# The last inverse pair of the first batch through DRAM instead of a direct table, four early units of the second batch, and low weight words on ScalarE

## The chip, the cores and the metric

The kernel runs on one core of one Trainium2 chip. The metric is the device time of one execution in microseconds (us), from three runs of the kernel before; the median is given. Profiled executions come with a trace of every instruction on TensorE (PE; its weight loads are PEld), VectorE (DVE), ScalarE (ACT), GpSimd (POOL) and SyncE (SP, which only issues DMAs).

## What is computed

```python
X = np.fft.rfft(x, axis=1)                  # x: 8 batches x 3008 rows x 256, float32
Y = X * (filt_r + 1j * filt_i)[None, :, :]
y = np.fft.irfft(Y, n=3008, axis=1).astype(np.float32)
t = y.reshape(8 * 3008, 256)                # 24064 tokens
h = t @ w_in                                # 256 -> 2048
g = h * np.clip(h + 3.0, 0.0, 6.0) / 6.0    # hard-swish
out = g @ w_out                             # 2048 -> 256
```

`w_in` and `w_out` come as float64 words; everything is computed in float32, so the kernel has to convert two 4 MB weights by itself, from pairs of 32-bit words.

## The kernel before

**Mixing.** The transform over 3008 = 47 x 64 rows is split into matrix products with small tables. For each batch after the first, `a_unit` (L433) makes the 47-point sums of four columns from `xs`, which `x_load` (L375) fetches with four SP DMAs; ScalarE copies one or both of its two PSUM banks to SBUF, `a_sums` (L447) does the rest on VectorE (for batch 1 one copy each for the last two units), and `z_store` (L456) writes the result to DRAM. `t2_load` fetches it transposed, `b_unit` (L479) makes the 64-point sums of two frequencies, `f_unit` (L499) multiplies by the filter on VectorE (three products of 128 x 512), `y_unit` (L513) adds the products, and `bi_unit` (L524) makes the inverse 64-point sums of a pair of units, which ScalarE copies out (L534) and `g_store` (L544, POOL's DMA queue) writes to DRAM (`g_tmp`). The inverse 47-point step reads it from there into `t4` and leaves tokens in the ring `xn`, of which the FFN takes blocks of 512. Batch 0 skips the first trip through DRAM: `a0_unit` (L403) and `turn` (L412, transposes on TensorE) do its first half. It also lets `bi_unit` take the filter's products directly, without `y_unit`, for all pairs but the last.

**The first block of tokens.** The first block needs only six groups of rows of batch 0. `first_load` (L575) fetches those six from `g_tmp` into `t4`, four SP DMAs at a time, for a stretch of frequencies. Frequencies 0 to 19 come this way, from the pairs that begin with units 0 to 8; for pair 8 `g0_first` (L537) writes just the six groups by four DMAs of 24 KB, two on ScalarE's queue and two on SP's. The last four frequencies (units 10 and 11) do not go through DRAM: `y_unit` adds their products on VectorE, and `direct` (L639) multiplies them by a table `direct_t` (128 x 4 x 564 float32, 1128 KB, loaded in the prologue) right into the PSUM tiles `psn`. `n_first` (L651) then adds the rest from `t4`, and ScalarE copies the result into `xn` (L658 to L662). Pair 10's inverse, wanted by later blocks only, runs between `direct` and `n_first` in the PSUM tiles `al` and `be`; pairs 8 and 10 are stored whole, on POOL's queue, after `n_first`.

**The FFN.** 47 blocks of 512 tokens, each of eight steps (256 hidden columns a step). Block 0 is multiplied plainly: `plain_up` (L784: L789, four matmuls for each half of a step), a relu on ScalarE (L726) and a product on VectorE (L731), then `plain_down` (L793: L800). Later blocks use a Strassen-Winograd form with fewer products (L681, L757), which needs sums of weights (`w_sums`, L356, 64 additions on POOL, and `w_scale`) and of tokens (`t_sums`, L671, POOL).

**Weights.** They come in 16 parts of 128 x 512 words in pairs (512 KB): `load_bits` fetches into whichever buffer is free, `w_abs` (L318) lets ScalarE take the magnitude of the high word (L321), and VectorE puts the float together (`w_conv`: L330, L332, L334 and, for the low word, L336; `w_conv_2`: L348, L350, L353). Low words are taken as a fraction between 1 and 2 by shift and mask, and L348 subtracts the 1 and multiplies. Part 0 is converted early, parts 1 to 3 between the first transform and block 0 (`w_abs` of 1 and 2 ahead of `direct`, of 3 after `n_first`), the rest in halves in steps 0 to 7 of block 0 (3, 3, 3, 4, 4, 3, 2, 2 halves). The tile of the magnitude has two buffers.

**What sets the order.** All of it is written out by hand: the whole runs under `tc.manual_schedule()`, each engine works its instructions off in the order in which the program issues them, and waits are put in for data and buffers. The prologue (L892 to L997) is straight code. From block 0 on a list `plan` holds what is done in each step; `at(step, fn, ...)` adds to it. `places(n)` (L1051) gives the steps for batch n's units; for batch 1: `a_unit` in steps 2 to 9, `b_unit` from step 12, `y_unit` from step 14. Steps 0 to 7 are block 0, 8 to 15 block 1.

Of the kernel before, what the change touches and what calls it, by code (L numbers as in the profile page):

```python
# [26 lines left out]
N = 3008  # L27
# [11 lines left out]
XC = 4  # L39
# [16 lines left out]
ATOM = 2 * KH  # L56
FIRST = tuple(range(NJ + 1, 0, -1))
# [19 lines left out]
def _make_tables():  # L77
# [76 lines left out]
    direct = np.zeros((P, TC, ND))  # L154
    for k in range(KH):
# [13 lines left out]
        if k >= KH - TC:  # L169
            for q in range(64):  # L170
                fr = k + NA * q if q < 32 else NA * (q - 31) - k
                for n, j in enumerate(FIRST):
                    th = [2 * np.pi * ((fr * rows(j, h, a)) % N) / N for h in range(2)]
                    direct[q, k - KH + TC, n * TOK:(n + 1) * TOK] = 2 / N * first_of(np.cos(th), n)
                    direct[HALF + q, k - KH + TC, n * TOK:(n + 1) * TOK] = -2 / N * first_of(np.sin(th), n)
    wai = np.concatenate([t.reshape(P, -1) for t in (groups, ones, first, last)], axis=1)
    f = np.float32
    return wa.astype(f), wai.astype(f), wb.astype(f), wi.astype(f), wf.astype(f), start.astype(f), direct.astype(f)
# [3 lines left out]
def kernel(  # L182
# [11 lines left out]
    wa_np, wai_np, wb_np, wi_np, wf_np, start_np, direct_np = _make_tables()  # L194
# [6 lines left out]
    direct_d = nc.inline_tensor(direct_np, name="direct_t").ap()  # L201
# [104 lines left out]
    def w_load(i, q):  # L306
        if W_AT[i] == "g":
            t = gp.tile([P, 7, 256], FP32, name="g")
            st["rest"] = t[:, 4:7, :].rearrange("p a n -> p (a n)")
            t = t.bitcast(I32)[:, 0:4, :].rearrange("p a n -> p (a n)")  # L310
        elif W_AT[i] == "x":
            t = xtp.tile([P, 5, PAIRS], FP32, name="xt").bitcast(I32)[:, 0:4, :].rearrange("p a n -> p (a n)")
        else:
            t = op.tile([P, 1024], I32, name="bits", tag="o")
# [3 lines left out]
    def w_abs(i):  # L318
        words = st["bits", i].rearrange("p (n two) -> p n two", two=2)
        st["high", i] = sp.tile([P, 512], FP32, name="s1")  # L320
        nc.scalar.activation(out=st["high", i], in_=words[:, :, 1].bitcast(FP32), func=AXT.Abs)  # L321


    def w_conv(i):
# [11 lines left out]
        v.tensor_scalar(out=lo, in0=lo, scalar1=9, scalar2=0x3F800000,  # L336
                        op0=ALU.logical_shift_right, op1=ALU.bitwise_or)

    def w_conv_2(i):
        big, rest, lo, hi = st.pop(("conv", i))  # L340
        v = nc.vector
        high = st.pop(("high", i), None)
        if high is None:
# [4 lines left out]
        v.scalar_tensor_tensor(out=rest, in0=lo.bitcast(FP32), scalar=1.0, in1=rest,  # L348
                               op0=ALU.subtract, op1=ALU.mult)
# [83 lines left out]
    def a_unit(b, c):  # L433
        xc = xs[:, (b * NB + c) % 3, :, :]
        t = t1p.tile([P, XC // 2, 2, D], FP32, name="t1")
        ps = [bank(b).rearrange("p (j d) -> p j d", d=D) for h in range(2)]
# [76 lines left out]
    def y_unit(b, i):  # L513
        s1, s2 = st["y", b, i]
        if b == 0 and i % 2 == 0:
            st["y0"] = t1p.tile([P, 2, 2, D], FP32, name="t1")
        y = yp.tile([P, 2, D], FP32, name="y") if b else st["y0"][:, i % 2, :, :]
# [6 lines left out]
    def bi_unit(b, i, ps=None):  # L524
        ys = [st.pop(("y", b, i + v)) for v in range(2)]
        ps = ps or [psF.tile([P, 2, D], FP32, name="psf", tag="f") for ri in range(2)]
        for v, ri in ((0, 0), (1, 0), (0, 1), (1, 1)):

            products = isinstance(ys[v], tuple)
            w, y = (wi[:, 1 + ri, :], ys[v][ri]) if products else (wi[ts(ri, 64), 0 if b else 3, :], ys[v][ts(ri, 64)])  # L530
# [6 lines left out]
    def g0_first(i):  # L537
        t = st["t3", 0, i]
        for v in range(2):
            for h in range(2):  # L540
                (nc.scalar, nc.sync)[v].dma_start(g_d[0, ds(h * HC + 1, NJ + 1), :, ds(2 * (i + v), 2), :].rearrange("c ri u d -> c ri (u d)"),
                                    t[ds(v * 64 + h * HC + 1, NJ + 1)].rearrange("p ri u d -> p ri (u d)"))

    def g_store(b, i):  # L544
        t = st.pop(("t3", b, i))
        for v in range(2):
            nc.gpsimd.dma_start(g_d[b, :, :, ds(2 * (i + v), 2), :].rearrange("c ri u d -> c ri (u d)"),  # L547
# [91 lines left out]
    def direct(i):  # L639
        if "psn" not in st:  # L640
# [547 lines left out]
```

## Time and profile before

| | us |
|---|---|
| median of 3 runs | 2660.89 (2660.49 to 2661.43) |
| the profiled execution | 2661.05 |
| its span in the trace | 2659.2 |
| TensorE busy | 2642.1 (99%) |
| VectorE busy | 2058.6 (77%) |
| ScalarE busy | 1306.3 (49%) |
| POOL busy | 495.1 (19%) |
| first matmul of block 0 (L789) | starts at 65.27 |
| first matmul of block 1 (L681) | starts at 129.30 |

The granted clock of TensorE is 1.0 over the span. A line of the page or of a group names the source line, the engine, the operation, the tile written and the tiles read; an arrow in square brackets says for how long the engine had been idle and what ended it. The chain of waits is followed back from the last instruction: each step is what released the one after it. A buffer may carry the name of an earlier tile in its place: `x0` and the direct table lie in the space of `w_all`, and so show up under that name.

### The profile page before, as it was taken

To read this page: it belongs to the slowest core of one execution; us is meant where nothing else is said; L and a number is where in the kernel's file an instruction comes from. 1 tells how busy PE (TensorE), PEld (TensorE's weight loads), DVE (VectorE), ACT (ScalarE), POOL (GpSimd) and SP (SyncE) were. 2 spreads that over 40 slices of the span, in tenths; PEclk is the share of its full clock that TensorE was granted. 3 is DMA by queue.
4 is the path that set the end of the run, shared out by engine and by line. 5 is a ranking of instruction groups with operands and counts; after the bars stand their busy time and mean duration, and the time that the engine had idled before them with its cause. 6 is when DMAs were issued, how large, how long until landed. Compare 5 with 4: busy or idle time off the path is not lost.

```text
span 2659.2 us, 54237 instructions
## 1 busy us (share of the span) xinstructions
PE 2642.1 (99%) x21584; PEld 2317.6 (87%) x21584; DVE 2058.6 (77%) x3503; ACT 1306.3 (49%) x2672; POOL 495.1 (19%) x731
## 2 busy tenths in 40 slices
PE   8999999999999999999999999999999999999999
PEld 6588888888888888888888888888888888899998
DVE  7978867877688876888768887688877878767666
ACT  3454444445545545455444545445455454454554
POOL 2252122111221112211031110311113120111110
PEclk9999999999999999999999999999999999999999
DMA  9732233212331123411223113231122421110000
GB/s 244 215 99 70 63 103 98 64 36 72 87 109 56 36 77 82 109 56 36 84 76 109 56 38 85 72 109 56 45 78 72 109 59 47 45 43 21 21 20 24
DMA packets 134818, 198.24 MB, mean 75 GB/s; under 512 B 23146, under 2 KB 99016, under 8 KB 134374
## 3 DMA queue, kind: packets, MB, share of 16 engines
q1 hardware_dynamic: 117037, 150.12, 19.8%
q0 software_dynamic: 16960, 44.16, 6.3%
q8 instruction: 170, 2.79, 0.4%
q14 instruction: 82, 0.67, 0.1%
q10 hardware_dynamic: 569, 0.50, 0.1%
HBM read 122.43 MB, written 83.98 MB: 78 GB/s over the span
## 4 chain that ended last, share of the span: by engine, by line
PE 95%; DVE 3%; DMA 1%; issue 0%; ACT 0%; SPq 0%; POOL 0%; POOLq 0%; DVEq 0%; ACTq 0%
PE po L757 43%; PE al L681 24%; PE be L681 18%; PE psn L621 2%; PE psf L531 2%; PE psf L440 2%; PE psf L487 1%; DVE g L731 1%; DMA w_all<-in_x_dram 0%; PE po L496 0%; PE po L800 0%; PE psn L632 0%; PE psf L496 0%; PE po L407 0%; DVE y L332 0%
## 5 line engine op out<-in xcount | busy, mean ns | idle before, releaser
L757 PEld LDWEIGHTS po<-w_all,g 128*128 128x128 f32 x10276 | 1362.3, 191 | 153.1 <-issue 44.1
L757 PE MATMUL po<-w_all,g 128*128 128x128 f32 x10276 | 1402.2, 276 | 0.2
L726 ACT ACTIVATE r<-h,half_c 128x512 f32<-128x512 f32 x736 | 531.0, 721 | 355.5 <-DVE h L707 343.5
L731 DVE SCALAR_TENSOR_TENSOR g<-r,h 128x512 f32<-128x512 f32 x736 | 531.3, 722 | 212.6 <-ACT r L726 200.3
L681 PE MATMUL al<-xt,w_all 128*128 128x256 f32 x2208 | 659.7, 381 | 0.1
L681 PE MATMUL be<-xt,w_all 128*128 128x256 f32 x1472 | 437.8, 379 | 0.0
L707 DVE TENSOR_TENSOR h<-be,s 128x512 f32<-128x512 f32 x368 | 253.9, 690 | 158.5 <-PE be L681 151.2
L681 PEld LDWEIGHTS al<-xt,w_all 128*128 128x128 f32 x2208 | 335.4, 192 | 1.0 <-POOL w_all L361 0.5
L681 PEld LDWEIGHTS be<-xt,w_all 128*128 128x128 f32 x1472 | 279.7, 190 | 37.9
L721 ACT ACTIVATE h<-al 128x256 f32<-128x256 f32 x368 | 141.4, 384 | 321.5 <-PE al L681 321.4
L712 DVE TENSOR_TENSOR h<-al,s 128x256 f32<-128x256 f32 x368 | 155.9, 424 | 150.2 <-PE al L681 149.1
L739 DVE TENSOR_TENSOR g<-g 128x512 f32<-128x512 f32 x367 | 261.4, 712 | 12.6
L702 ACT ACTIVATE s<-al 128x256 f32<-128x256 f32 x368 | 141.4, 384 | 194.5 <-PE al L681 191.1
L547 POOL DMA_DIRECT2D g_tmp<-t x96 | 55.3, 592 | 937.7 <-ACT t L534 937.7
L693 ACT ACTIVATE s<-be 128x256 f32<-128x256 f32 x368 | 141.4, 384 | 176.3 <-PE be L681 176.3
L681 PE MATMUL al<-xn,w_all 128*128 128x256 f32 x736 | 222.4, 384 | 1.4 <-DVE h L712 1.4
L681 PE MATMUL be<-xn,w_all 128*128 128x256 f32 x736 | 218.9, 379 | 0.0
L677 POOL TENSOR_TENSOR xt<-xn 128x256 f32<-128x256 f32 x184 | 135.8, 756 | 434.4 <-ACT xn L603 434.4
L738 DVE TENSOR_TENSOR g<-g 128x256 f32<-128x256 f32 x367 | 172.5, 470 | 12.5
L692 ACT ACTIVATE s<-al 128x256 f32<-128x256 f32 x368 | 141.4, 384 | 68.2 <-PE al L681 68.2
L741 DVE TENSOR_TENSOR g<-g 128x256 f32<-128x256 f32 x367 | 159.8, 435 | 12.5
L461 POOL DMA_DIRECT2D z_tmp<-t x192 | 95.2, 504 | 365.0 <-DVE t L454 347.6
(149 smaller groups left out, 1845.8 us busy)
## 6 DMA issues: line engine op xcount, KB each, us to landing
g_tmp<-t POOLq DMA_DIRECT2D x96, 256.0 KB, 3.7
t<-g_tmp SPq DMA_DIRECT2D x184, 120.0 KB
t<-z_tmp SPq DMA_DIRECT2D x42, 512.0 KB
z_tmp<-t POOLq DMA_DIRECT2D x192, 96.0 KB, 2.5
xs<-in_x_dram SPq DMA_DIRECT2D x112, 128.0 KB
o_tmp<-o SPq DMA_DIRECT2D x46, 256.0 KB
ft<-in_filt_r_dram SPq DMA_DIRECT2D x168, 64.0 KB
ft<-in_filt_i_dram SPq DMA_DIRECT2D x168, 64.0 KB
```

The source lines that it names most:

```text
L681: nc.tensor.matmul(ps, w_in[p][:, w, :], x, start=start, stop=stop, skip_group_check=True)
L692: nc.scalar.activation(out=s[:, 0, :], in_=al, func=AXT.Copy)
L693: nc.scalar.activation(out=s5, in_=be[:, 1, :], func=AXT.Copy)
L702: nc.scalar.activation(out=s[:, 1, :], in_=al, func=AXT.Copy)
L707: nc.vector.tensor_tensor(out=st["h"][0].rearrange("p (a n) -> p a n", a=2), in0=be, in1=s, op=ALU.add)
L712: nc.vector.tensor_tensor(out=st["h"][1][:, 256:512], in0=al, in1=s5, op=ALU.add)
L726: nc.scalar.activation(out=r, in_=st["h"][i], func=AXT.Relu, bias=half_c, scale=1.0 / 6.0)
L731: nc.vector.scalar_tensor_tensor(out=st["g", k, p][:, o:o + 2, :].rearrange("p a n -> p (a n)"), in0=st["r", i], scalar=1.0, in1=st["h"][i ...
L738: v.tensor_tensor(out=g[:, G1, :], in0=g[:, G3, :], in1=g[:, G22, :], op=ALU.add)
L739: v.tensor_tensor(out=g[:, G3:G2 + 1:2, :], in0=g[:, G3:G1 + 1, :], in1=g[:, G11:G11 + 1, :].broadcast_to([P, 2, 256]), op=ALU.subtract)
L741: v.tensor_tensor(out=g[:, G4, :], in0=g[:, G12, :], in1=g[:, G2, :], op=ALU.subtract)
L757: nc.tensor.matmul(st["po", k][bank][:, part, u, :], g[:, a, ts(u, P)], w_out[p][:, w, :], start=(p == 0 and n in OPENS and u == 0), stop= ...
```

## The change

1. The direct table, its two loads, `direct` and batch 0's `y_unit`s are taken out. The last pair's inverse now takes the filter's products, as for the other pairs.
2. Pairs 8 and 10 of batch 0 are stored whole (two DMAs of 256 KB each) on SP's queue. A third `first_load` fetches the last four frequencies, and `n_first` makes all of the first block's inverse from `t4`, with one PSUM bank (`bank(0)`) for the sixth group of both halves.
3. Four `a_unit`s of batch 1 are moved ahead of block 0: one before pair 10's inverse, three between its store and the third `first_load`; three write their results into `t2` tiles, and all four use `po` banks. Their z stores go to POOL's queue. The x loads and the table `wa` (now whole) are issued earlier on SP's queue. The other four `a_unit`s stand in steps 0, 2, 3 and 5; the first `b_unit`s and `y_unit`s of batch 1 are moved forward by up to three steps.
4. `w_abs` of part 3 is moved up, before the first early `a_unit`.
5. For parts 1 to 15, L336 on VectorE is replaced by an activation on ScalarE (copy of the low word, read as uint32, times 2^-32), and L348 becomes a plain product. `half_c`, the relu's bias, is made in the same way from a word of 0x80000000.

```diff
-            st["rest"] = t[:, 4:7, :].rearrange("p a n -> p (a n)")
...
         nc.scalar.activation(out=st["high", i], in_=words[:, :, 1].bitcast(FP32), func=AXT.Abs)
+        nc.scalar.activation(out=words[:, :, 0].bitcast(FP32), in_=words[:, :, 0].bitcast(mybir.dt.uint32), func=AXT.Copy, scale=2.0 ** -32)
...
-        v.tensor_scalar(out=lo, in0=lo, scalar1=9, scalar2=0x3F800000,
-                        op0=ALU.logical_shift_right, op1=ALU.bitwise_or)
+        if ("high", i) not in st:
+            v.tensor_scalar(out=lo, in0=lo, scalar1=9, scalar2=0x3F800000,
+                            op0=ALU.logical_shift_right, op1=ALU.bitwise_or)
...
+        if direct:
+            v.tensor_tensor(out=rest, in0=lo.bitcast(FP32), in1=rest, op=ALU.mult)
+        else:
+            v.scalar_tensor_tensor(out=rest, in0=lo.bitcast(FP32), scalar=1.0, in1=rest,
+                                   op0=ALU.subtract, op1=ALU.mult)
...
-        t = t1p.tile([P, XC // 2, 2, D], FP32, name="t1")
-        ps = [bank(b).rearrange("p (j d) -> p j d", d=D) for h in range(2)]
+        if b == 1 and c < EARLY_A - 1:
+            t = t2p.tile([P, TC, D], FP32, name="t2").rearrange("p (j s) d -> p j s d", s=2)
+        else:
+            t = t1p.tile([P, XC // 2, 2, D], FP32, name="t1")
+        ps = [bank(b > 1 or c >= EARLY_A).rearrange("p (j d) -> p j d", d=D) for h in range(2)]
...
     def n_first():
-        for (c, dh), ps in st.pop("psn").items():
-            for q, j in enumerate(chunks[c][1]):
-                nc.tensor.matmul(ps[:, ts(q, TOK)], t4[:, j - 1, ts(dh, P)], edges[:, FIRST.index(j), :],
-                                 start=False, stop=True, skip_group_check=True)
...
+        one = bank(0).rearrange("p (e n) -> p e n", e=2)
+        for dh in range(2):
+            for c in range(2):
+                ps = one[:, dh, :] if c else psF.tile([P, 512], FP32, name="psn", tag="f")
+                for q, j in enumerate(chunks[c][1]):
+                    nc.tensor.matmul(ps[:, ts(q, TOK)], t4[:, j - 1, ts(dh, P)], edges[:, FIRST.index(j), :],
+                                     start=q == 0 and c * dh == 0, stop=True, skip_group_check=True)
...
+        nc.vector.memset(top_c, -0x80000000)
+        nc.scalar.activation(out=half_c, in_=top_c.bitcast(mybir.dt.uint32), func=AXT.Copy, scale=2.0 ** -32)
         nc.vector.memset(top_c, -0x40000000)
-        nc.vector.memset(half_c, 0.5)
...
-        last = x0_at(HC * D - 2048, 3 * ND)
-        nc.sync.dma_start(last, direct_d[:, 0:3, :].rearrange("p k n -> p (k n)"))
         load_bits(3)
-        st["direct"] = [last[:, ts(k, ND)] for k in range(3)] + [st["rest"][:, 0:ND]]
-        nc.sync.dma_start(st["direct"][3], direct_d[:, 3, :])
...
-                if c == NT - 1:
-                    y_unit(0, i)
...
                 bi_unit(0, 2 * c - 2)
-                (g0_first if c == NT - 1 else lambda i: g_store(0, i))(2 * c - 2)
+                g_store(0, 2 * c - 2, nc.gpsimd if c < NT - 1 else nc.sync)
+            if c == 1:
+                nc.sync.dma_start(wa, wa_d)
             if c == 4:
+                for j in range(3):
+                    x_load(1, j)
                 first_load(0, KH - 3 * TC)
+        for i in 1, 2, 3:
+            w_abs(i)
+        a_unit(1, 0)
+        x_load(1, 3)
         first_load(KH - 3 * TC, KH - TC)
-        for i in 1, 2:
-            w_abs(i)
-        direct(NU - 2)
-        direct(NU - 1)
-
-        bi_unit(0, NU - 2, [psU.tile([P, 512], FP32, name=n).rearrange("p (u d) -> p u d", u=2) for n in ("al", "be")])
+        bi_unit(0, NU - 2)
+        g_store(0, NU - 2, nc.sync)
+        for j in range(1, EARLY_A):
+            a_unit(1, j)
+        x_load(1, EARLY_A)
+        first_load(KH - TC, KH)
+        for j in range(EARLY_A):
+            z_store(1, j, nc.gpsimd)
         load_bits(6)
-        nc.sync.dma_start(wa[:, 0:528], wa_d[:, 0:528])
         nc.sync.dma_start(wf, wf_d)
         n_first()
-        g_store(0, NU - 4)
-        g_store(0, NU - 2)
-        for c in range(2):
-            x_load(1, c)
-            load_bits(7 + c)
-        w_abs(3)
+        x_load(1, EARLY_A + 1)
+        load_bits(8)
         convert(3)
...
-                return (list(range(2, NB + 2)), [12, 13, 15, 18, 19, 20, 22, 23, 26, 27, 28, 30],
-                        [14, 15, 16, 19, 21, 22, 24, 25, 27, 29, 30, 31], [16, 21, 24, 29, 31, 32])
+                return (list(range(2 - EARLY_A, 2)) + [0, 2, 3, 5], [9, 12, 14, 18, 19, 20, 22, 23, 26, 27, 28, 30],
+                        [13, 15, 16, 19, 21, 22, 24, 25, 27, 29, 30, 31], [16, 21, 24, 29, 31, 32])
```

## The prediction

> **What bounds the kernel now.** I read the page first, busy shares and then the chain of the work that ended last.
>
> ```profile
> PE 2642.1 (99%) x21584; PEld 2317.6 (87%) x21584; DVE 2058.6 (77%) x3503; ACT 1306.3 (49%) x2672; POOL 495.1 (19%) x731
> PE 95%; DVE 3%; DMA 1%; issue 0%; ACT 0%; SPq 0%; POOL 0%; POOLq 0%; DVEq 0%; ACTq 0%
> ```
>
> TensorE bounds the span. Of 2659.2 us only the first 190 or so hold anything that the diff touches, so the question is when block 1 starts, after which TensorE has no gaps, and what work lies in it. Next I cut the chain of waits at 45 to 70 us, where the last inverse pair hands over to the first block (start, length, what):
>
> ```profile
> 51.08 0.61 ACT t L534
> ...
> 51.71 4.35 DMA g_tmp<-t
> ...
> 56.08 2.33 DMA g_tmp<-t
> ...
> 58.74 3.25 DMA t<-g_tmp
> ...
> 62.08 2.46 PE psn L654 x20
> 64.56 0.47 ACT xn L658
> 65.03 0.20 ACT xn L661
> ...
> 65.27 1.98 PE al L789 x4
> ```
>
> The chain does not run through the direct products. They lie on TensorE from 52.03 to 60.6 (timeline, 8.6 us), under the trip of pair 8 through DRAM. `n_first` waits for that trip until 62.08. So removing the products frees no time here; what counts is how long the trip of pair 10 takes, and from when.
>
> Last, the busy time of each engine by stretch (stretch; length, PE, PEld, DVE, ACT, POOL, clock, DMA share, GB/s):
>
> ```profile
> 80.00:90.00 10.00, 10.00 (x59) 5.62 (x58) 9.48 (x18) 4.38 (x7) 0.00 (x0) 1.00 0.92 215
> ...
> 100.00:110.00 10.00, 10.00 (x56) 6.37 (x50) 9.69 (x14) 4.37 (x8) 6.05 (x7) 1.00 0.21 54
> ```
>
> In block 0, VectorE (weight conversion and hard-swish) is as full as TensorE: 9.5 to 9.7 of 10 us. ScalarE is at 44% and has room.
>
> **What the Trainium skill says.** "TensorE: Matmul & The Clock Gate", Part 1 (The HAM clock gate): after an idle window of about 3.4 us TensorE runs at half rate until it has been busy for as long. The trace agrees. The last matmul ends at 2653.17 us, and the granted clock then reads
>
> ```profile
> 2656.00:2657.00 1.00, 0.00 (x0) 0.00 (x0) 0.00 (x0) 0.00 (x0) 0.00 (x0) 1.00 0.31 76
> 2657.00:2658.00 1.00, 0.00 (x0) 0.00 (x0) 0.00 (x0) 0.00 (x0) 0.00 (x0) 0.76 0.00 0
> 2658.00:2659.20 1.20, 0.00 (x0) 0.00 (x0) 0.00 (x0) 0.00 (x0) 0.00 (x0) 0.50 0.00 0
> ```
>
> so it fell some 4.4 us after it. At the start, four 128x512 matmuls of L939 take 3.78 us where L789's four take 1.98 and 1.88, and the slow rate lasts from 2.78 to about 8.86, 6.1 us. The same page (Architectural detail) says that ScalarE and VectorE work off their queues strictly in order. The trace agrees: a ScalarE conversion step waits 5.00 us for its load, and the relu behind it, whose matmul ended at 105.80, waits with it:
>
> ```profile
> 107.28 0.70 ACT L321 ACTIVATE s<-bits 128x512 f32<-128x512 f32 x1 [5.00 <-DMA bits<-in_moe_w_out_dram]
> 107.89 0.67 ACT L726 ACTIVATE r<-al,half_c 128x512 f32<-128x512 f32 x1
> ```
>
> "VectorE: DVE Perf Modes", The perf-mode tier table: an fp32 tensor_scalar in SBUF has a double-rate mode, an fp32 tensor_tensor has not. The trace agrees in kind, 0.42 us for L336 against 0.69 for the two-tensor L348:
>
> ```profile
> 81.25 0.42 DVE L336 TENSOR_SCALAR bits<-bits 128x512 int32<-128x512 int32 x1
> 81.71 0.69 DVE L348 SCALAR_TENSOR_TENSOR y<-bits,y 128x512 f32<-128x512 f32 x1
> ```
>
> The change takes the cheap one, L336, off VectorE and leaves L348 a two-tensor operation. Start to start, L334 takes 0.34 and L336 0.46 us; L348 needs the last result before it either way, so I keep the 0.46 and count 0.34 saved a part (bounds 0.34 and 0.46).
>
> **Part 1, the hand-over.** The built order of ScalarE after the copies of pair 8 is: L321 and the new low-word copy for parts 1, 2 and 3, two copies of `a_unit(1, 0)`, two copies of pair 10 (L534). Part 3's L321 needs a buffer of two that part 1 holds until VectorE ends its conversion (L353). VectorE: the products of unit 11 started at 51.96 behind two `y_unit` operations of 0.72 which are gone, so they start at 50.52 and end at 52.7; conversion 1 then takes 3.83 (4.17 now, from 79.67 to 83.84, less 0.34 for L336) and ends at 56.5. Behind this wait stand, in order: L321 and the low-word copy of part 3, 1.2 us (L321 takes 0.65 to 0.72; the new copy has the same shape, no row of its own, and I bound it by 0.57, an L321's pitch, and 0.72) to 57.8; `a_unit(1, 0)`'s copies, 0.53 each (1.06 for two of L443), to 58.85; pair 10's copies, 0.6 each, to 60.0. That pair's inverse has long been done (its inputs are ready at 52.7).
> From 60.0 the store goes out on SP in two DMAs, 0.5 us of issue each. I take 3.0 us for the second to land: at least the 2.33 of the 24 KB store above, at most the 5.9 that is the median of the 256 KB POOL stores between 44 and 68 us. So 60.0 + 0.5 + 3.0 = 63.5. Meanwhile SP issues four x loads (2.15 us for four of L380), which are done by then. Four loads of the last rows follow: three issues ahead at 0.5, then 3.25 as in the chain above, 68.2. From `n_first` to L789 it takes 3.2 us now (62.08 to 65.27): 71.4. **+6.15 us**, bounds +4.5 (store 2.33, loads nearer 2.3 us) and +9 (store 5.9).
> The sixteen z stores (POOL, 0.50 us of issue each by L461's 95.2 us for 192) and the x loads are issued in the same stretch; POOL has nothing else then. They weigh on the upper bound.
>
> **Part 2, the clock.** TensorE's last work ahead of the fetch is `a_unit(1, 3)`, near 61.7, as its banks wait for ScalarE's copies. Up to 68.2 are 6.5 us, more than 4.4. I expect half rate from `n_first` on, for 6.1 us less some 0.5 in which TensorE waits for copies anyway, of which half is lost: **+2.8**, bounds 0 (the window falls kindly) and 4.1.
>
> **Part 3, block 0.** From its first L789 (65.27) to block 1's first matmul (129.30) it takes 64.03 us. In it, TensorE works about 60.6: eight ups of 3.53, seven downs of 3.56, six `a_unit`s of 1.02, one inverse step of 1.31. VectorE ends the conversion that POOL's sums wait for at 125.36, 60.09 after the start. The change takes eleven L336 at 0.34 of pitch from it (3.7) and adds two copies of `a_sums` at 0.69, which move in from steps 8 and 9 (1.4). 60.09 − 3.7 + 1.4 = 57.8; I give back 0.45 for low-word copies that stand ahead of a relu on ScalarE, 58.25; POOL's first sums and TensorE's last down take 3.2 more, so block 1 starts at 61.5: **−2.55**. Bounds: −1.5 (each low-word copy holds up a relu and VectorE with it) and −5.9 (TensorE alone bounds: 60.6 less two `a_unit`s is 58.55, less 0.45 if an inverse step overlaps).
>
> **Part 4, block 1.** Two `a_unit`s (steps 8 and 9) are gone from it: 2 × 1.02, and 0.15 of gaps beside them, **−2.2**.
>
> **At nothing.** The low-word copies after block 0's start: 0.6 us for each of a dozen parts on an engine that is 44% busy; uncovered, they are bounded in part 3. `half_c` by ScalarE: TensorE's first products wait for x0 until 15.7; uncovered, one activation, 0.7. The direct table's 1128 KB and its first POOL stores leave the DMA queues early, where SP's weight loads wait for nothing on the chain: 0, or 0.7 gained in the load term, inside its bound.
>
> **Sum.** 6.15 + 2.8 − 2.55 − 2.2 = +4.2 on the profiled execution's 2661.05 us is 2665.25. The median of the runs, 2660.89, lies 0.16 below that execution: 2665.1.
>
> **Rivals.**
> - B, TensorE keeps its clock: 2665.1 − 2.8 = 2662.3, and 2660.6 if the trip takes its lower bound as well. For it: `a_unit`s that finish later than I think would break the gap. Against: 6.5 is well over 4.4.
> - C, block 0 becomes bound by TensorE and the clock stays: −5.9 in place of −2.55, so 2659.0, and 2657.3 with the short trip. For it: VectorE enters block 0 without a backlog (now conversion 3 runs until 68.3, three us into the block). Against: even then VectorE has 57.8 us of work to the gate, near TensorE's 58.55, and two engines that are both full stall each other.
> - D, slower: the trip through DRAM runs in crowded queues. Between 62 and 65 the queues move 390 GB/s now; the z stores add 1.5 MB there. With the store at 5.9 (+2.9) and 0.9 more on the loads, 2665.1 + 3.8 = 2668.9. It decides from a trip 1.1 us longer than I take.
> - The low words may not relieve VectorE: if it waits for ScalarE instead, block 0 keeps its length but for 1.5, which is A's upper end.
>
> **Chances.** A, the sum as it stands, 0.50, own range 2662.5 to 2667.5; B 0.25, 2660 to 2663; C 0.10, 2655 to 2659.2; D 0.15, 2667.5 to 2671. What a measurement can tell from no change is 0.2%, 5.3 us: 2655.6 and 2666.2. Slower: D and a third of A, 0.31. Faster: the lower half of C, 0.05. Same: 0.64. The range 2659.2 to 2669.0 leaves out C and about half of D.
>
> **What would show it.** Right: in the chain, ScalarE's copies of pair 10 end near 60.0 behind part 3's L321, the last load lands near 68, and L789 starts near 71.4; the clock reads under 1.00 at 68 to 73; block 1 starts some 61.5 us later (64 if the half rate falls in it); VectorE is still over 9 of 10 in block 0; TensorE gap-free after it. Wrong: `n_first` before 66 (ScalarE's wait did not matter), a full clock there, or block 0 much under 60 us.

## The result, and the profile after

| | before | after |
|---|---|---|
| median, us | 2661.16 (4 runs) | 2680.68 (4 runs, 2677.74 to 2680.98) |
| ratio, 95% interval | | 1.0073 (1.006 to 1.0085) |
| profiled execution's span | 2659.2 | 2678.9 |
| `n_first` starts | 62.08 | 75.89 |
| first L789 (after: L773) | 65.27 | 81.61 |
| first matmul of block 1 | 129.30 | 150.23 |

The changed kernel is 19.5 us slower; 4.2 had been predicted. Medians and ratios below are of undisturbed executions: of z_late's four, one took 5482.81 us and is left out. All line numbers from here on are those of the changed kernel: L636 is `n_first`'s L654 of before, L773 the ups' L789, L784 the downs' L800, L538 and L570 the stores to and fetches from `g_tmp`, L312 and L313 the two conversion steps on ScalarE. First the page: the busy shares are the same to a per cent, and TensorE's busy time rises by 1.5 us only, while the span grows by 19.7. So most of the loss is time in which TensorE waits; what it loses at half rate is hidden in the busy time, from which the direct products are gone.

```profile
PE 2643.6 (99%) x21552; PEld 2318.6 (87%) x21552; DVE 2050.3 (77%) x3484; ACT 1318.1 (49%) x2688; POOL 501.3 (19%) x743
PE 94%; DVE 3%; DMA 2%; issue 0%; ACT 0%; SPq 0%; POOL 0%; POOLq 0%; DVEq 0%; ACTq 0%
```

The chain of waits at the hand-over (start, length, what), in place of the one of before:

```profile
61.98 8.54 DMA g_tmp<-t
...
71.96 3.79 DMA t<-g_tmp
...
75.89 2.42 PE psn L636 x10
...
78.73 2.15 PE psn L636 x10
...
80.90 0.57 ACT xn L640
...
81.61 3.78 PE al L773 x4
```

Pair 10's store takes 8.54 us to land, where 3.0 had been taken. `n_first` lasts 5.7 us instead of 3.2 from its start to L773, and the first matmuls of L773 take 3.78 instead of 1.98. SP's queue shows when things were issued (its timeline: start, length, line, tile), and the DMA issues of 60 to 80 us show what was under way beside the store (number, KB each, us to landing):

```profile
55.08 1.27 SPq L538 DMA_DIRECT2D g_tmp<-t  x2
56.85 2.29 SPq L377 DMA_DIRECT2D xs<-in_x_dram  x4
59.95 1.36 SPq L570 DMA_DIRECT2D t<-g_tmp  x4
61.42 1.18 SPq L538 DMA_DIRECT2D g_tmp<-t  x2
```

```profile
z_tmp<-t POOLq DMA_DIRECT2D x14, 96.0 KB, 7.2
```

Pair 8's fetch (59.95) stands between pair 8's store (55.08) and pair 10's (61.42). The z stores of the early units, 96 KB each, take 7.2 us to land; the page of before has 2.5 for their kind.

A second wait is new, in block 0. The chain there, and TensorE's clock by stretches (length, PE, PEld, DVE, ACT, POOL, clock, DMA share, GB/s):

```profile
104.48 0.45 SPq L377
...
104.99 5.22 DMA xs<-in_x_dram
...
110.34 2.91 PE psf L440 x16
113.25 5.32 PE po L784 x16
```

```profile
57.00:58.00 1.00, 0.00 (x0) 0.00 (x0) 0.90 (x2) 1.00 (x3) 0.00 (x0) 1.00 0.98 239
58.00:59.00 1.00, 0.78 (x6) 0.48 (x10) 0.92 (x2) 1.00 (x3) 0.06 (x1) 0.79 0.93 315
59.00:60.00 1.00, 1.00 (x12) 0.54 (x7) 0.97 (x2) 1.00 (x4) 1.00 (x3) 0.50 0.76 238
...
85.00:86.00 1.00, 1.00 (x3) 0.37 (x2) 0.00 (x0) 0.56 (x1) 0.00 (x0) 0.56 0.00 0
86.00:87.00 1.00, 1.00 (x4) 0.35 (x2) 0.69 (x1) 0.12 (x1) 0.00 (x0) 1.00 0.00 0
...
110.00:111.00 1.00, 0.66 (x2) 0.29 (x2) 0.96 (x2) 0.00 (x0) 0.00 (x0) 0.50 1.00 297
```

An x load that SP issues only at 104.48, behind weight loads (L306), ends TensorE's wait of 3.27 us at 110.34. The clock is at half from 58.6 to 85.9, and again from 109.8 to 116.6: there an `a_unit` of 1.09 us takes 2.91, a down of 3.72 takes 5.39. The first fall comes before the long gap at the hand-over, in an early `a_unit` for whose banks TensorE had waited 1.93 us:

```profile
58.23 2.46 PE L440 MATMUL po<-xs,wa 47*64 47x256 f32 x16 [1.93 <-ACT t L443]
```

VectorE is as full as before until the wait at 110.34, and has room after it:

```profile
100.00:110.00 10.00, 7.07 (x24) 4.39 (x24) 9.59 (x17) 4.74 (x8) 0.00 (x0) 0.99 0.96 265
110.00:120.00 10.00, 9.66 (x36) 6.30 (x37) 7.08 (x12) 2.83 (x5) 0.00 (x0) 0.67 0.24 82
```

The conversion itself does what the change says. ScalarE's low-word copy takes 0.67 us, and L343, the product that follows on VectorE, 0.69 as L348 before; once it waits 0.28 us for that copy:

```profile
90.04 0.67 ACT L313 ACTIVATE xt<-xt 128x512 f32<-128x512 uint32 x1
```

```profile
90.75 0.69 DVE L343 TENSOR_TENSOR y<-xt,y 128x512 f32<-128x512 f32 x1 [0.28 <-ACT xt L313]
```

### The profile page after: what moved, and what is told of

The parts are those of the page before. It is cut to its first block, busy times and chain, and to the rows that moved or that the text cites. A ratio compares the mean times of both kernels' runs of the same rounds, so it can differ in the third digit from the quotient of the medians.

```text
span 2678.9 us, 54160 instructions
## 1 busy us (share of the span) xinstructions
PE 2643.6 (99%) x21552; PEld 2318.6 (87%) x21552; DVE 2050.3 (77%) x3484; ACT 1318.1 (49%) x2688; POOL 501.3 (19%) x743
## 3 DMA queue, kind: packets, MB, share of 16 engines
q1 hardware_dynamic: 116681, 148.49, 19.5%
## 4 chain that ended last, share of the span: by engine, by line
PE 94%; DVE 3%; DMA 2%; issue 0%; ACT 0%; SPq 0%; POOL 0%; POOLq 0%; DVEq 0%; ACTq 0%
PE po L741 43%; PE al L665 24%; PE be L665 17%; PE psn L612 2%; PE psf L440 2%; PE psf L529 2%; PE psf L487 1%; DVE g L715 0%; DMA ft<-in_filt_i_dram 0%; PE psf L496 0%; PE po L784 0%; PE psn L623 0%; DMA g_tmp<-t 0%; DMA wa<-wb_t 0%; DMA w_all<-in_x_dram 0%
## 5 line engine op out<-in xcount | busy, mean ns | idle before, releaser
L538 POOL DMA_DIRECT2D g_tmp<-t x92 | 53.2, 593 | 925.0 <-ACT t L532 922.3
L461 POOL DMA_DIRECT2D z_tmp<-t x208 | 103.2, 504 | 377.7 <-DVE t L454 348.7
```

## The experiments

Theory 1, rival D of the prediction in a stronger form: the early units' transfers hold up pair 10's trip, and the waiting costs TensorE its clock. Rival theory 2: SP's queue and its x loads hold it up, not the z stores. Rival 3: ScalarE's part in the change (the wait for part 3, the low words) is what costs. All runs in one table. The ratio is against the kernel before, run again in the same session (medians from 2660.66 to 2661.36); the last three columns come from each one's own profile. Starts of one prologue differ by up to 3.6 us between profiles, so lengths say more than starts; and a profile is one execution, which can lie 2.4 us from its run's median (fixed6, whose profiled execution is the longest of 18).

| run | median us | ratio (95%) | `n_first` | first L773 | block 0, us |
|---|---|---|---|---|---|
| (before) | 2661.16 | | 62.08 | 65.27 | 64.03 |
| (changed kernel) | 2680.68 | 1.0073 (1.006 to 1.0085) | 75.89 | 81.61 | 68.62 |
| z_late | 2675.30 | 1.0055 (1.0038 to 1.0072) | 70.24 | 75.96 | 68.30 |
| x4_late | 2679.81 | 1.0069 (1.0054 to 1.0084) | 74.66 | 80.39 | 69.84 |
| quiet | 2676.70 | 1.0060 (1.0045 to 1.0075) | 72.00 | 77.72 | 69.41 |
| warm | 2678.63 | 1.0070 (1.0054 to 1.0087) | 75.93 | 79.34 | 67.84 |
| x6_early | 2676.81 | 1.0058 (1.0043 to 1.0073) | 77.09 | 82.82 | 63.77 |
| no_low | 2685.12 | 1.0085 (1.007 to 1.01) | 77.16 | 82.89 | 72.07 |
| low_only | 2659.36 | 0.9994 (0.9985 to 1.0002) | 63.05 | 66.24 | 62.47 |
| low_abs3 | 2659.61 | 0.9992 (0.9984 to 1.0000) | 61.42 | 64.61 | 62.47 |
| no_early | 2670.67 | 1.0035 (1.0022 to 1.0048) | 67.16 | 72.89 | 64.09 |
| abs3_late | 2670.88 | 1.0035 (1.0023 to 1.0047) | 68.99 | 74.72 | 64.24 |
| trip | 2668.05 | 1.0025 (1.0015 to 1.0035) | 65.45 | 71.18 | 64.52 |
| no_early_warm | 2668.09 | 1.0027 (1.0016 to 1.0038) | 70.47 | 73.89 | 62.46 |
| trip_warm | 2668.05 | 1.0028 (1.0017 to 1.0039) | 66.23 | 71.95 | 63.88 |
| trip_warm13 | 2663.98 | 1.0011 (1.0004 to 1.0017) | 67.17 | 70.58 | 62.47 |
| fixed3 | 2670.42 | 1.0033 (1.0019 to 1.0046) | 71.69 | 77.42 | 63.84 |
| fixed4 | 2674.62 | 1.0047 (1.0034 to 1.0061) | 79.67 | 82.85 | 61.77 |
| fixed5 | 2668.45 | 1.0028 (1.0017 to 1.0038) | 67.82 | 73.37 | 63.98 |
| fixed6 | 2667.56 | 1.0023 (1.0016 to 1.0030) | 70.70 | 74.54 | 66.73 |

### The transfers: z_late, x4_late, quiet

```diff
         first_load(KH - TC, KH)
-        for j in range(EARLY_A):
-            z_store(1, j, nc.gpsimd)
...
         load_bits(8)
+        for j in range(EARLY_A):
+            z_store(1, j, nc.sync)
```

> The changed kernel, with the sixteen z stores of the four early units issued on SP's queue after n_first's loads instead of on POOL's queue at 59 us. Theory 1 (the z stores crowd the DMA engines, so that pair 10's store takes 8.54 us to land): the store lands in 3 to 4 us, n_first starts near 71, the first L773 near 76, the time falls by 5 to 6 us to about 2675. Theory 2 (the x loads ahead on SP's queue and their traffic are what holds the store and the fetch): the landing stays over 7 us and the time within 1.5 us of 2680.7.

```diff
-        x_load(1, EARLY_A)
         first_load(KH - TC, KH)
+        x_load(1, EARLY_A)
```

> The changed kernel, with the x load of unit 4 (four DMAs, 376 KB) issued after the last fetch instead of before it. Theory 1 (z stores crowd the queues): the store still lands after 7 us or more, and the time falls by 1.5 us at most, to 2679 or above. Theory 2 (x loads): the fetch is issued near 66 instead of 70.6, n_first starts near 71 and the time falls by 4 to 6 us to about 2675.

Quiet has both edits.

> Both moves together: z stores and the x load of unit 4 after the last fetch. Floor of the trip with nothing of the early units in its way: store issued at 61.4 to 62.6, landed near 65, fetch issued to 66.6, landed near 70; n_first near 70, first L773 near 74.5 (the clock is still half, since TensorE idles from 63.5 for over 6 us). Under theories 1 and 2 together 2672 to 2674; if the trip stays at 8 us or more here too, both are wrong and the store itself (256 KB from 64 partitions in two DMAs) is what is slow.

The chain of z_late, then the store in that of x4_late:

```profile
61.11 3.96 DMA g_tmp<-t
...
65.79 3.89 DMA t<-g_tmp
...
70.24 2.42 PE psn L636 x10
```

```profile
62.62 6.94 DMA g_tmp<-t
```

With the z stores gone, the store lands in 3.96 us instead of 8.54, and the first L773 comes 5.65 us earlier; the median falls by 5.4, as expected. With only the x load moved it still takes 6.94, and the median falls by 0.9, inside the spread of the runs. Quiet, at 2676.70, gains no more than z_late and misses the 2672 to 2674 expected of it; its profile began the trip later (`n_first` at 72.00), and block 0 took longer. Theory 1 holds against theory 2 for the landing: with the sixteen stores of 96 KB beside it, it takes more than twice as long. Z_late moves them to another time and to another queue; which of the two counts is not shown.

### The clock and the late x load: warm, x6_early

Warm puts idle products on TensorE in the gap, x6_early moves one load. Both edits are shown together; the `ps` and `keep_warm` lines are warm's, the others x6_early's:

```diff
+        ps = psU.tile([P, 512], FP32, name="al")
+        keep_warm(9)
         n_first()
         x_load(1, EARLY_A + 1)
+        x_load(1, EARLY_A + 2)
...
-                if c >= (3 if n > 1 else EARLY_A + 2):
+                if c >= (3 if n > 1 else EARLY_A + 3):
```

> The changed kernel, with nine idle products (128x512, two matmuls each, of zeros into a PSUM tile that nothing reads) on TensorE between the last early unit and n_first, so that it does not idle there. If the half clock after the gap costs what the trace suggests (n_first 5.7 instead of 3.2 us, and 1.9 more in the first step), T0 comes 2.5 us earlier and the time falls by 4 to 4.5 us to about 2676.3. If the clock is not what makes them slow, or block 0 is bound by VectorE and takes it back, less than 2 us.

> The changed kernel with the x load of unit 6 issued right behind that of unit 5, ahead of block 0, instead of in step 1. Theory (late x load): the 3.3 us wait of TensorE in step 3 and the half clock of the 8 us after it are gone, block 0 falls from 68.6 to 62 or 63 us, the time by 5.5 to 7 us to about 2674.5. Rival (block 0 is bound by VectorE anyway, which the wait only hides): less than 2 us.

In warm the first L773 comes 2.3 us earlier with `n_first` where it was. The clock had fallen before the idle products, at 58.9, and was back at 69.1, still during them. The median falls by 2.1, half of what was expected; in block 0 TensorE then waits 5.0 us for the late x load instead of 3.3. In x6_early that wait and the half clock behind it are gone, block 0 takes 63.77 us (of them 1.75 in the half clock of its first step: 6.66 us between the first two al products, against 3.89 before and 1.02 for the unit between), and the median falls by 3.9. It was to fall by 5.5 to 7: in its profile the trip began 1.2 us later, and a smaller wait appears, two us at the next inverse step (TensorE's timeline, then VectorE's):

```profile
118.61 1.38 PE L612 MATMUL psn<-wai,t 48*64 48x47 f32 x78 [2.09 <-DVE t L451]
```

```profile
117.88 0.68 DVE L451 COPY t<-psf 128x512 f32<-128x512 f32 x1
```

L451 is `a_sums`' copy of unit 6. It empties the PSUM bank that the inverse step is to have and stands on VectorE behind two parts' conversion.

### ScalarE: no_low, low_only, abs3_late

No_low takes the low words back to VectorE in the changed kernel, low_only puts them on ScalarE in the kernel before. The core of no_low, which low_only has the other way round (the tests in `w_conv` and `w_conv_2` go with it):

```diff
-        nc.scalar.activation(out=words[:, :, 0].bitcast(FP32), in_=words[:, :, 0].bitcast(mybir.dt.uint32), func=AXT.Copy, scale=2.0 ** -32)
...
-            v.tensor_tensor(out=rest, in0=lo.bitcast(FP32), in1=rest, op=ALU.mult)
...
+        v.scalar_tensor_tensor(out=rest, in0=lo.bitcast(FP32), scalar=1.0, in1=rest,
+                               op0=ALU.subtract, op1=ALU.mult)
```

> The changed kernel with the low words back on VectorE (L336 as before). Theory (block 0 is bound by the x load of unit 6, which waits on SP behind loads that are issued when conversions end): conversions take 0.34 us longer each, so the x load is issued about 1.4 us later and block 0 gets 2 to 4 us longer: 2682 to 2685. Rival (ScalarE's low-word copies cost time ahead of block 0 and ahead of relus): the time falls, to 2679 or less.

> The kernel before with the low words alone done by ScalarE (direct products, g0_first and the places of all units as before). If VectorE's conversion bounds block 0, as part 3 of the prediction has it: eleven parts at 0.34 us, less what TensorE then bounds, so block 0 in 61 to 62.5 us instead of 64.0 and the time 1.5 to 3 us lower, about 2658.5. Rival (low words are given back as waits of relu and VectorE for ScalarE): within 0.5 us of 2660.7.

The low words are a gain in both: taking them back costs 4.4 us in the changed kernel, where SP's x load waits for conversions to end, and adding them takes 1.9 off the kernel before (block 0 from 64.03 to 62.47). TensorE then has two gaps in block 0, of 0.6 and 0.7 us: it bounds, and more relief of VectorE can give little. The ratio's interval just includes 1, so the gain over the kernel before is likely and not certain. Rival 3 falls for the low words.

For the wait for part 3 there is a kernel with its early units taken out (no_early: all eight `a_unit`s, their loads and stores placed as before the change; the rest of the change stays), and one with that wait moved as well (abs3_late, the `w_abs` lines):

```diff
-EARLY_A = 4
+EARLY_A = 0
...
-        for i in 1, 2, 3:
+        for i in 1, 2:
             w_abs(i)
...
         g_store(0, NU - 2, nc.sync)
+        w_abs(3)
```

> The changed kernel without early units: all a_units of batch 1 in steps 2 to 9 with their x loads and z stores as in the kernel before; the direct products stay out, and pair 10 goes through DRAM. Nothing of the units stands in the trip then: pair 8 is stored at 51.7, pair 10 near 59, landed near 63, n_first near 68, at half clock, first L773 near 73.5, block 0 near 62 us: about 2666 to 2668. If the trip of pair 10 were slow for a reason of its own, n_first would stay near 75 and the time over 2675. If part 3's wait on ScalarE did not matter and SP's order did, n_first comes near 65 and the time near 2664.

> The kernel without early units, with part 3's conversion on ScalarE behind pair 10's copies; SP's order as in the change (pair 8's fetch ahead of pair 10's store). If ScalarE's wait set the trip's start (prediction, part 1): as trip, 2668. If SP's order did: no change from 2670.7, since the store waits behind pair 8's fetch, which waits for pair 8's store to land.

No_early takes 10.0 us off the changed kernel; 2666 to 2668 had been expected, but block 0 took 64.09 us where 62 had been taken. Its trip is near the one that the prediction worked out, with `n_first` at 67.16 against 68.2 on record:

```profile
58.02 0.51 SPq L538
...
58.57 3.21 DMA g_tmp<-t
...
67.16 2.42 PE psn L636 x10
```

Moving ScalarE's wait out of the way gains nothing (2670.88 against 2670.67). The chain of abs3_late and the waits on SP (in all, times, longest) say why:

```profile
53.91 3.90 DMA g_tmp<-t
...
57.95 0.28 SPq L570
...
59.05 0.30 SPq L570
...
59.45 0.51 SPq L538
...
60.01 3.53 DMA g_tmp<-t
```

```profile
SPq L570 <- DMA g_tmp<-t: 7.9, 4, 3.3
```

Pair 10's copies are done at 56.6 there, but its store waits on SP behind pair 8's fetch, which waits for pair 8's store to land. In no_early it was ScalarE that was late, by a microsecond: the copies end at 58.00, and SP is free from 56.97 on.

### The order on SP, and the clock alone: trip, trip_warm, trip_warm13, no_early_warm

```diff
-        for i in 1, 2, 3:
+        for i in 1, 2:
             w_abs(i)
-        first_load(KH - 3 * TC, KH - TC)
         bi_unit(0, NU - 2)
         g_store(0, NU - 2, nc.sync)
+        w_abs(3)
+        first_load(KH - 3 * TC, KH - TC)
```

This is trip, an edit of no_early. The other three add idle products: trip_warm seven and trip_warm13 thirteen to trip, no_early_warm fourteen to no_early.

```diff
+        ps = psU.tile([P, 512], FP32, name="al")
+        keep_warm(7)
         n_first()
```

> The kernel without early units, with part 3's conversion on ScalarE moved behind pair 10's copies, and pair 10's store ahead of pair 8's fetch on SP's queue. If ScalarE's wait and SP's order hold the trip up (prediction, part 1): the store is issued near 55 instead of 58, n_first starts near 63.5 instead of 67.2, and the time falls by 3 to 4 us to about 2667. If pair 8's fetch is what is late next: n_first near 66 and 1 us or less.

> The kernel without early units, with fourteen idle products on TensorE between pair 10's inverse and n_first. n_first stays near 67; it takes 3.2 instead of 5.7 us and the first step 3.6 instead of 5.2. If nothing takes that back: 4 us off, about 2666.5. If block 0 is bound by VectorE or by loads, only part of it: 2668 or more.

> As the run before, with seven idle products on TensorE ahead of n_first. If both gains add up, n_first near 63.5 at full clock, first L773 near 66.7, block 0 near 62.6 as in the run with the low words alone: about 2660 to 2662, no faster than the kernel before, since the trip of pair 10 starts after that of pair 8 and can't end before it. If the clock does not matter here: 2665 or more.

> As the run trip_warm, with thirteen idle products instead of seven, so that TensorE is busy until shortly before n_first. If the half clock costs what the traces suggest (n_first 5.7 instead of 3.2 us, the first step 5.6 instead of 3.6): first L773 near 69 and the time 4 to 4.5 us below trip's 2668.05, about 2664. If block 0 takes it back: 2666 or more.

With pair 10's store ahead of the fetch (and part 3 moved), the median falls by 2.6, less than the 3 to 4 expected: the stores are issued from 52.4 to 56.4, but from the fetch's last issue to `n_first` it takes 4.8 us there, in no_early 4.0. Trip_warm failed as a test: its idle products end too early, and the clock falls all the same. Six more of them cover the gap (TensorE's timelines of trip_warm, then trip_warm13):

```profile
54.20 6.28 PE L924 MATMUL al<-r 128*128 128x512 f32 x14
66.23 2.42 PE L636 MATMUL psn<-wai,t 128*128 128x94 f32 x10 [5.76 <-DMA xt<-in_moe_w_in_dram]
```

```profile
55.50 11.43 PE L924 MATMUL al<-r 128*128 128x512 f32 x26
67.17 1.32 PE L636 MATMUL psn<-wai,t 128*128 128x94 f32 x10 [0.24 <-DMA xt<-in_moe_w_in_dram]
```

`n_first`'s first ten products take 2.42 us in one and 1.32 in the other, and the median is 4.1 us lower: the price of one half clock here, since the two kernels differ in nothing but idle products. No_early_warm, with 2.6, shows less because its executions differ: three of the seven took 2665.4 to 2665.9 us, at a mean clock of 1.000, three 2670.5 to 2671.6, at 0.998, and the profiled one 2668.09, at 0.999 (its one half-rate stretch lies in the prologue, from 18.2 to 21.6). So its idle products, which leave 1.94 us idle in the profile, seem to hold the clock in some executions and not in others. Trip_warm13 has all of the change but its early units, with its order mended. It is still slower than the kernel before, by 2.6 us, and by 4.6 than low_only, which has the same low words and the direct products.

### All mended: fixed3, fixed4, fixed5, fixed6

These keep the four early units. Fixed3 joins z_late, x6_early and idle products (three behind pair 10's inverse, six ahead of `n_first`). Fixed4 adds trip's order and x4_late, and has eight idle products ahead of `n_first`. Its order, where it differs from the changed kernel (the old places of the moved lines are not shown):

```diff
         a_unit(1, 0)
+        bi_unit(0, NU - 2)
+        keep_warm(3)
+        g_store(0, NU - 2, nc.sync)
+        w_abs(3)
         first_load(KH - 3 * TC, KH - TC)
+        x_load(1, 3)
         for j in range(1, EARLY_A):
             a_unit(1, j)
         first_load(KH - TC, KH)
         x_load(1, EARLY_A)
```

Fixed5 takes unit 3 and its load behind `n_first` and the last fetch, with seven idle products there instead of fixed4's eight; fixed6 has nine.

```diff
-        x_load(1, 3)
-        for j in range(1, EARLY_A):
+        for j in range(1, EARLY_A - 1):
             a_unit(1, j)
         first_load(KH - TC, KH)
+        x_load(1, 3)
         x_load(1, EARLY_A)
...
-        keep_warm(8)
+        keep_warm(7)
         n_first()
+        a_unit(1, EARLY_A - 1)
```

> The changed kernel with three repairs together: z stores after the last fetch, the x load of unit 6 ahead of block 0, and idle products on TensorE (three behind pair 10's inverse, six ahead of n_first) against the half clock. If the three causes are separate and add up (4.4, 3.9 and 2 to 4.4 us by the runs so far): 2668.5 to 2670.5, with n_first near 70.5, first L773 near 73.8 and block 0 near 62. If one only hides another, 2672 or more.

> The changed kernel with its four early units and all that was found mended: z stores and x loads of units 4 to 6 after the last fetch, part 3's conversion behind pair 10's copies, pair 10's store ahead of pair 8's fetch, and idle products (three behind pair 10's inverse, eight ahead of n_first). If these are all the causes: n_first near 68 at full clock (the first x loads still go ahead of pair 8's fetch, 3 us), first L773 near 71.5, block 0 near 61 to 62 and two units less in block 1: 2663 to 2665. If something else is lost in it: 2667 or more.

> As the run fixed4, with the fourth early unit and its x load moved behind the last fetch and n_first (in fixed4 its load went out behind pair 8's fetch and TensorE waited for it at 67.36, at half clock, ahead of n_first), and seven idle products instead of eight. If the causes found are all there are: n_first near 68.5 at full clock, first L773 near 72.5, block 0 near 61.5 and two units less in block 1: 2663 to 2666. If the time stays over 2669, something in the early units costs that has not been found.

> As the run fixed5, with nine idle products instead of seven ahead of n_first. In fixed5 they ended 1.75 us before n_first, and the clock fell at 69.8 all the same, for some 7 us of work. If that half clock is what fixed5 still lost: no clock under 1.00 between 64 and 80, 3 to 3.5 us off, about 2665. If not: 2667.5 or more.

Fixed3's 2670.42 is at the upper end of what adding up was to give, with 4.4 us counted for z_late; with its 5.4 the sum is 1 us lower, and fixed3 falls short of it. The clock fell in it 2.2 us after the last idle product. Fixed4 was spoilt by its own edit:

```profile
67.36 2.85 PE L440 MATMUL po<-xs,wa 47*64 47x256 f32 x16 [6.20 <-DMA xs<-in_x_dram]
70.14 9.53 PE L924 MATMUL al<-r 128*128 128x512 f32 x16
```

TensorE waits 6.2 us for the x load of unit 3, falls to half rate, and the idle products, at twice their length, then stand ahead of `n_first`. Fixed5 takes that away (6.2 us off) but misses the 2663 to 2666 expected. Fixed6 holds the clock at 1.00 from 62 to 84, for 0.9 us, inside the spread, where 3 to 3.5 were expected. Its profile, of its longest execution, has new losses in their place, and how much of them the other executions have is not known: the last fetch, with eight x-load DMAs issued behind it, takes 5.7 us, and in block 0 conversion waits for its bits, and with it `a_sums`' copy and the inverse step, after which the clock is at half for 6.8 us (VectorE, then TensorE):

```profile
105.12 0.43 DVE L322 TENSOR_SCALAR y<-xt 128x512 int32<-128x512 int32 x1 [2.88 <-DMA xt<-in_moe_w_in_dram]
```

```profile
111.28 2.29 PE L612 MATMUL psn<-wai,t 48*64 48x47 f32 x78 [5.04 <-DVE t L451]
```

So the causes found are not all that can go wrong with the early units: in these profiles a transfer that was put off lay beside another that was due. No version with them has a median below 2667.

### A version better than both

Low_abs3 is low_only with part 3's two ScalarE steps ahead of pair 10's copies:

```diff
-        for i in 1, 2:
+        for i in 1, 2, 3:
             w_abs(i)
         direct(NU - 2)
...
-        w_abs(3)
         convert(3)
```

> The kernel before with the low words on ScalarE and part 3's magnitude and low word ahead of pair 10's copies instead of after n_first, where VectorE waited for them. Theory: the first steps of block 0 lose their wait for VectorE (0.6 us on TensorE), 0.5 to 1 us below the run with the low words alone: 2658.5, and with five rounds clearly below the kernel before. Rival: TensorE alone bounds block 0 by now, or the copies of pair 10 come late: no change, 2659.4.

It is as fast as low_only (2659.61), not faster: block 0 takes 62.47 us in both. The wait of 0.6 us for VectorE in it was not removed, it moved: from 70.55 in low_only to 75.83 here, about a step later in the block. These two are the best kernels of the study, 0.06 to 0.08% below the kernel before, at the edge of what the runs resolve.

## Why the prediction was wrong, step by step

The profiled spans differ by 19.7 us, which the traces divide as follows:

| term | predicted | measured | from |
|---|---|---|---|
| the hand-over, to `n_first` | +6.15 | +13.8 | 75.89 − 62.08 |
| the clock, after that gap | +2.8 | +4.4 | `n_first` to L773 5.72 against 3.19; first step 6.76 − 1.02 (a unit) against 3.89 |
| block 0 without that | −2.55 | +2.7 | 68.62 − 64.03 − 1.85 |
| block 1 on | −2.2 | −1.2 | (2678.9 − 150.23) − (2659.2 − 129.30) |
| sum | +4.2 | +19.7 | |

- **The hand-over.** The failed step is "I take 3.0 us for the second to land", with "at most the 5.9": it was 8.54, beyond the upper bound, and z_late (3.96) shows that the z stores do it. Of the 7.7 us by which the hand-over exceeds the prediction, 5.5 are this landing, 1.5 the store's later issue (its landing counts from 61.98 instead of 60.5), 0.7 the fetch. The prediction named the z stores as what would "weigh on the upper bound", and its rival D, which has their traffic as the cause, got 15%. Rival D is the right mechanism, with half its size. In no_early, where they are absent, `n_first` comes within about a microsecond of the estimate.
- **ScalarE's head-of-line wait.** Its times came true (pair 10's copies ended at 59.6, 60.0 predicted), but it was not the last thing that the store waited for: in the changed kernel SP got to the store only at 61.42, behind four x loads and pair 8's fetch, and abs3_late shows that with ScalarE's wait gone SP's order takes back what is gained. The prediction read the order of ScalarE closely but laid no clock along SP's ahead of the store. An engine that only issues DMAs has a path of its own, and in the changed kernel this one was the longer.
- **The clock.** Half rate after `n_first` came as forecast, in part by luck, and the term was mis-sized. The prediction had the clock fall in the gap behind the last early unit, as that gap is longer than 4.4 us; it had fallen at 58.6, after an idle 1.93 us that the prediction does not have, and was still down when the gap of 12.3 us began. From `n_first` on half rate lasted 10.0 us (75.89 to 85.9) where 6.1 had been taken from the start of the kernel. Trip_warm13 gives 4.1 for one.
- **Block 0.** The relief is there: low_only, with the low words alone and six units in block 0, has −1.56; x6_early, with four units, 63.77 − 1.75 = 62.0, so −2.0 against −2.55, with a wait of 2.09 still in it. A part now takes VectorE 3.84 us (79.97 to 83.81 in low_only) where it took 4.17, 0.33 less, as the prediction had it. What failed is that the x loads moved with the units were followed only as far as the first L773. The load of unit 6 stands in step 1 behind loads that SP issues when conversions end; it was issued at 104.48 and took 5.22 us beside 512 KB weight loads. It cost 3.3 us of waiting and 3.5 of a second half clock (2.91 − 1.09, 5.39 − 3.72), 6.8 in all. The prediction had no line for it.
- **Block 1.** Two units less, 2.05 as worked out; 0.8 of it is lost to a wait of TensorE for VectorE at 192.69, which the kernel before does not have.
- **Removing the direct products.** The prediction held that this frees no time, and that their place is the shade of pair 8's trip. Trip_warm13 against low_only agrees: without the products, and with the clock held, the kernel is no faster but 4.6 us slower, the price of the second trip in the best version that was tried.

The Trainium skill's "TensorE: Matmul & The Clock Gate", Part 1, on which the clock term rests, agrees in kind, and less closely than the prediction says. Its windows of some 3.4 us would let one expect a fall after 3.4 us of idle time and a recovery of one window or a little more. Here 1.93 us of idle time were enough (1.75 in fixed5), and from the first product after the hand-over's gap the recovery took 10.0 us in the changed kernel, 9.0 in z_late and no_early, 8.6 in trip_warm, 10.0 in fixed3; after the second fall of the changed kernel it took 6.3 (110.34 to 116.6). The measurement decides. What makes some recoveries longer than others is not shown.

The product that replaces L348 takes 0.69 us like it, as the prediction expects with "VectorE: DVE Perf Modes". Of the two lines that it compares there, L336 is an int32 operation, so they do not test what that table says of fp32 operations.

What stays open: how the wait of 5.04 us in fixed6 and the slower fetch there divide among the loads beside them; no run takes those loads apart.

## What to carry to other kernels

Work that is put into an idle gap of the busiest engine brings its transfers along: lay every DMA that it issues, and the ones that it displaces, along the queue for as long as they are under way, and look for a transfer that is on the chain in that stretch. A wait that empties TensorE for some microseconds is paid twice, with the half clock that follows: the late x load cost 3.3 us of waiting and 3.5 of half rate. And test the parts of a change one by one: of this one, only the low words on ScalarE, which bring no transfer along, gained, and that by 1.9 us, at the edge of what the runs resolve.

## What the runs showed of the hardware

The clock can fall after a shorter idle time than the 4.4 us seen at the end of the kernel before. In fixed3 TensorE is idle from 69.23 to 71.69, and the clock is half from 71.4 on, for 10.2 us; in no_early_warm it is idle from 68.53 to 70.47 and keeps its clock (the same columns as above):

```profile
70.00:71.00 1.00, 0.00 (x0) 0.00 (x0) 0.00 (x0) 0.00 (x0) 0.00 (x0) 1.00 0.97 190
71.00:72.00 1.00, 0.31 (x2) 0.34 (x2) 0.00 (x0) 0.00 (x0) 0.00 (x0) 0.70 1.04 385
...
81.00:82.00 1.00, 1.00 (x3) 0.52 (x2) 0.04 (x1) 0.69 (x1) 0.00 (x0) 0.68 0.75 250
82.00:83.00 1.00, 1.00 (x3) 0.19 (x1) 0.65 (x1) 0.00 (x0) 0.00 (x0) 1.00 0.64 209
```

```profile
69.00:70.00 1.00, 0.00 (x0) 0.00 (x0) 0.00 (x0) 0.00 (x0) 0.00 (x0) 1.00 1.08 379
70.00:71.00 1.00, 0.53 (x5) 0.56 (x6) 0.00 (x0) 0.00 (x0) 0.00 (x0) 1.00 0.98 369
```

In the changed kernel an idle time of 1.93 us was enough, in fixed5 one of 1.75, while no_early_warm's 1.94 was not. So the length of the gap alone does not decide. The times of the changes say more. In the changed kernel they are 58.58, 85.88, 109.78 and 116.60: 27.30, 23.90 and 6.82 us apart, which is 8, 7 and 2 steps of 3.413 us. In all twenty profiles every stretch between two changes is a whole number of such steps. The steps do not start with the gap: in fixed3 2.17 us of the gap lie in one step (67.99 to 71.40), at whose end the clock falls, and in no_early_warm the end of a step, at 69.39, divides the gap into 0.85 and 1.07. That fits a clock set by how busy TensorE was in the step just ended; how much idle time a step bears was not measured. For a kernel it means that a gap of about two microseconds can go either way, and that idle products have to reach near its end: trip_warm's stopped 5.76 us early and gained nothing, trip_warm13's 0.24 us early.

A store of 256 KB landed in 3.2 to 4.0 us in the four runs where the z stores came later and pair 8's fetch still went ahead of it (no_early, abs3_late, quiet, z_late). Beside sixteen stores of 96 KB it took 8.5, while the queues moved 216 GB/s from 60 to 70 us, with the DMA engines busy for 0.81 of it; between 62 and 65 us of the kernel before they moved 390. So the store was held up well below the rate that the queues can move; what held it is not shown.
